# Another order of all engines' steps, from a search over four sets of transfer times

## The chip, the core and the metric

The kernel runs on one core of a Trainium2 chip. The metric is the device time of one execution in microseconds (us). The engines are TensorE (PE in the profile, its weight loads PEld), VectorE (DVE), ScalarE (ACT), GpSimd (POOL) and SyncE (SP), which here only issues transfers.

## What is computed

One transformer layer on x of 2048 rows by 512 columns, bf16: attention with 32 heads of 16 over a dilated window of 8 rows (the row itself and those 2, 4, ..., 14 before), then a gated feed-forward of width 1376, each behind a layer norm and with a residual.

```python
off = jnp.arange(W) * dil                     # W = 8, dil = 2
idx = pos[:, None] - off[None, :]             # rows before the first are masked
logits = jnp.einsum("bhsd,bhswd->bhsw", q, kg) * scale
attn = _softmax(jnp.where(mask, logits, -1e9), axis=-1)
o = jnp.einsum("bhsw,bhswd->bhsd", attn, vg)
...
h = x + _A_ref(_layernorm(x), A_wqkv, A_wo)
gate, up = hn @ W_gate, hn @ W_up             # hn = _layernorm(h)
h2 = h + (relu(gate) * up) @ W_down
```

## The kernel before, in words

The 2048 rows go in four chunks of 512 (0 to 3). For each chunk:

1. Layer norm of x, four blocks of 128 rows: statistics (L466, L469) on VectorE, the normalised rows on VectorE (L501) or ACT (L498). The rows are then transposed so that columns lie on the partitions: chunks 0 to 2 on TensorE (L530, evicted at L546), chunk 3 by four DMA transposes that SP issues (L519). The result is one `quad` buffer for each chunk.
2. Projections on TensorE (L571): twelve groups of four matmuls, 128x512 each, four groups for q, four for k and four for v, each evicted by ACT (L579).
3. Products of q and shifted k on VectorE (L619; in halves, L634, in chunk 0), their sums over a head's columns on TensorE (L625, 16 matmuls for a half, that is for four of the eight window rows), Exp on ACT (L683). In chunk 0 a mask is put on the weights' first columns (L686).
4. SP broadcasts a half's weights to all partitions in four transfers (L743, `big<-ex`). VectorE multiplies them with shifted v (L775; in halves, L790, in chunk 0) and adds the eight window rows in a tree. The first level of the tree, eight rows to four, is done in chunks 0 to 2 by an accumulating DMA that GpSimd issues (L818, 512 KB, `big<-big`), the others by VectorE (L778, L782 or L812).
5. Output projection on TensorE (L854; in chunk 0 the residual is added there, L857, and ACT evicts with a row sum, L863), layer norm of h (L447, L455, L501), feed-forward (L927, evicted at L931 and L934, products at L955) and down projection (L977) with the output. Chunks 0 and 1 add the residual by an accumulating DMA of GpSimd (L1011), 2 and 3 on VectorE (L990).

All four chunks overlap, so one engine's queue holds steps of several chunks. Every step is an `Op` with an engine. The table `RANK` has one number for each of the 744 steps; `Plan.order` sorts each engine's steps by it (SP's and GpSimd's too), and then replays the queues with assumed durations, one step at a time. Each engine thus executes its steps strictly by rank: where the next one must wait, all behind it wait. The assumed durations (of loads `XT` and `WT`, of engine operations `MM`, `SW`, `A5` and so on) no longer set the order within an engine. They only decide which of several equal buffers a step takes, the one that is assumed free first, and how the engines' steps stand among each other in the program's text.

Of the kernel before, what the change touches and what calls it, by code (L numbers as in the profile page):

```python
# [8 lines left out]
P = 128  # L9
# [3 lines left out]
ACT = mybir.ActivationFunctionType  # L13
ALU = mybir.AluOpType
# [188 lines left out]
def kernel(  # L203
# [11 lines left out]
    nc = tc.nc  # L215
    Bsz, S, D = A_x.shape
# [3 lines left out]
    NT = D // P  # L220
# [7 lines left out]
    PRD = ()  # L228
    ODA = (0, 1)
# [12 lines left out]
    HB = P // 4  # L242
# [53 lines left out]
    V = nc.vector  # L296
# [67 lines left out]
    add = plan.add  # L364
# [8 lines left out]
    TDD, TDL = 1.25, 1.5  # L373
    NWARM, NFILL = 56, (13, 10, 0)
    NHALF = 6
    XT = (3.55, 3.4, 6.1, 5.85, 9.0, 9.3, 9.6, 10.0, 15.2, 16.75)
    WT = (7.7, 7.7, 5.6, 12.05, 18.0, 24.95, 21.45, 28.8)
# [4 lines left out]
    BDI = {"S": 0.63, "A": 0.65, "P": 0.95}  # L382
# [16 lines left out]
    MM, TP = 0.2165, 0.057  # L399
    SW = 0.21  # L400
    PEL = 0.22
    A5, A10, AX, AS = 0.485, 0.91, 0.75, 0.21
    AL = 0.13
    D2, D5, D10, D20, D40, DST, DSM = 0.33, 0.61, 0.60, 1.14, 2.2, 0.61, 0.09
    DXN = 0.33
    DL = 0.12
# [147 lines left out]
    for tk in range(NCK):  # L554
# [50 lines left out]
        for hf in range(2):  # L605
            sc, ex = Buf(at_s), Buf(ex_s)
            scd, prd = [], []
            for t in range(0, NT, 2):
# [13 lines left out]
                def f_sc(t=t, sc=sc, pb=pb):  # L622
                    for u in range(2):
                        for g in range(4):
                            nc.tensor.matmul(sc.t[g * HB:(g + 1) * HB, :], lhsT=sel[:],  # L625
                                             rhs=pb.t[:, 4 * u + g, :], start=(t + u == 0),
                                             stop=(t + u == NT - 1), tile_position=(0, g * HB))
# [13 lines left out]
                else:  # L641
                    a = add(("pr%d" % hf, tk), "DVE", D40, f_pr, [d[k] for k in (t, t + 1) for d in (qd, kd, kp)],
                            apr, take=[pb], use=[qT], lat=DL)
                    prd.append((a, pb, f_sc))
# [29 lines left out]
            elif tk in MERGE:  # L674
                scd = [add(("sc%d" % hf, tk), "PE", 4 * MM + SW, lambda p=prd: [f() for _, _, f in p],
                           [a for a, _, _ in prd], apr, take=[sc], use=[b for _, b, _ in prd], lat=PEL)]
            else:
                for a, pb, f in prd:
                    scd.append(add(("sc%d" % hf, tk), "PE", 2 * MM + SW, f, [a] + scd[-1:], apr,
                                   take=[sc], use=[pb], lat=PEL))  # L680
# [52 lines left out]
        for w0 in range(0, W, BCN):  # L733
            hf = w0 // 4
            if (tk, hf) in BCD:
                for eng, q in (("SP", nc.sync), ("ACT", nc.scalar), ("POOL", nc.gpsimd)):
# [4 lines left out]
                    def f_bd(ws=ws, q=q, w0=w0, ab=ab, ex=exs[hf]):  # L741
                        for w in ws:
# [3 lines left out]
                                   take=[ab], use=[exs[hf]], lat=0.77,  # L746
# [102 lines left out]
        for j in range(BPC):  # L849
# [20 lines left out]
            if tk in RPE:  # L870
                a = add(("rs%d" % j, tk), "ACT", 0.57, f_rs, [a], base + 50, take=[sm], use=[od], lat=AL)
            else:
                a = add(("rs%d" % j, tk), "DVE", 0.63, f_rs, [a], base + 50, take=[sm], use=[od], lat=DL)
# [190 lines left out]
```

## Time and profile before

| what | us |
| --- | --- |
| median of 3 runs | 197.8 (197.04 to 198.03) |
| profiled execution (its span, from the first to the last instruction) | 199.0 |
| TensorE busy | 189.6 |
| VectorE busy | 147.9 |
| ACT busy | 116.7 |

The profiled execution is one run, 1.2 us over the median. In the views below, times are from the start of the span. A line such as `PE bank L571` is the work on TensorE that line 571 issues into a `bank` of PSUM. What stands in brackets behind a row of the timeline is the idle time ahead of it on its engine and what ended that. A busy TensorE in the profile is an upper bound, since a matmul's end is modelled. In a row of windows the busy times of PE, PEld, DVE, ACT and POOL follow each other, then the granted share of the TensorE clock, the share of DMA engines that were busy and GB/s.

### The profile page before, as it was taken

What the parts mean: (1) busy time and instruction counts of PE and PEld (TensorE: products, weight loads), DVE (VectorE), ACT (ScalarE), POOL (GpSimd) and SP (SyncE); (2) the same over time, 40 slices, a digit from 0 to 9 for tenths busy, and PEclk for the clock granted to TensorE, in tenths of its full rate; (3) what the DMA queues carried; (4) which work ended last, traced back from release to release, by engine and by line L of the source; (5) the groups of instructions that cost most, each with busy time, mean ns of one, the idle gap of its engine ahead of it and who ended that gap; (6) DMA issues with size and microseconds to landing.
All of it is one profiled execution on the core that took longest, in us unless ns stands there. A gap on an engine that the chain in (4) does not pass through costs nothing.

```text
span 199.0 us, 3083 instructions
## 1 busy us (share of the span) xinstructions
PE 189.6 (95%) x1120; PEld 98.5 (50%) x1139; DVE 147.9 (74%) x239; ACT 116.7 (59%) x241; POOL 17.7 (9%) x35
## 2 busy tenths in 40 slices
PE   8899998599999999999999999999999999999992
PEld 8895455245445534554444445544454544455451
DVE  6889999969969999999998769999954311214322
ACT  3579999326779676775536659606458725146300
POOL 3000002520000003300024010010010010000000
PEclk9999999879999999999999999999999999999999
DMA  6889386999600535967379973360030454000303
GB/s 207 231 274 381 96 183 126 190 187 350 217 0 0 137 78 105 190 127 160 80 146 174 188 174 65 65 120 3 0 53 8 103 178 110 0 0 0 109 6 126
DMA packets 25070, 24.61 MB, mean 124 GB/s; under 512 B 11136, under 2 KB 21344, under 8 KB 25056
## 3 DMA queue, kind: packets, MB, share of 16 engines
q1 hardware_dynamic: 22032, 16.23, 29.7%
q0 software_dynamic: 2304, 7.34, 20.2%
q10 hardware_dynamic: 720, 0.85, 1.2%
q8 instruction: 9, 0.15, 0.3%
q14 instruction: 5, 0.04, 0.1%
HBM read 8.42 MB, written 2.10 MB: 53 GB/s over the span
## 4 chain that ended last, share of the span: by engine, by line
PE 90%; DMA 5%; ACT 1%; issue 1%; DVE 1%; ACTq 0%
PE bank L927 34%; PE bank L571 20%; PE bank L977 19%; PE bank L854 7%; PE bank L625 4%; PE bank L894 3%; DMA quad<-row 3%; DMA x_sm<-in_A_x_dram 2%; PE bank L530 1%; ACT quad L579 1%; PE bank L857 0%; PE bank L700 0%; DVE st L466 0%; ACT lnd L706 0%; ACTq L319 0%
## 5 line engine op out<-in xcount | busy, mean ns | idle before, releaser
L927 PE MATMUL bank<-quad,wgu_sb 128*128 128x512 bf16 x311 | 72.0, 379 | 0.4
L927 PEld LDWEIGHTS <-wgu_sb 128*128 128x128 bf16 x320 | 31.0, 98 | 36.5 <-issue 0.8
L977 PE MATMUL bank<-wd_sb,gT 128*128 128x512 bf16 (+2 forms) x185 | 40.4, 367 | 0.2
L571 PE MATMUL bank<-quad,wqk_sb 128*128 128x512 bf16 (+1 forms) x149 | 31.2, 358 | 3.5 <-DMA quad<-row 3.1
L931 ACT CAST up_sb<-bank 128x512 bf16<-128x512 f32 x40 | 22.8, 589 | 19.5 <-PE bank L927 15.9
L934 ACT ACTIVATE gr<-bank 128x512 bf16<-128x512 f32 x40 | 23.3, 601 | 17.6 <-PE bank L927 10.9
L619 DVE TENSOR_TENSOR big<-quad,kT 128x4096 bf16<-128x4096 bf16 x12 | 27.2, 2284 | 2.4 <-ACT quad L579 2.2
L977 PEld LDWEIGHTS <-gT 128*128 128x128 bf16 (+1 forms) x187 | 18.1, 98 | 19.7 <-issue 0.4
L775 DVE TENSOR_TENSOR big<-big,vT 128x4096 bf16<-128x4096 bf16 x12 | 27.1, 2284 | 0.4 <-issue 0.2
L571 PEld LDWEIGHTS <-wqk_sb 128*128 128x128 bf16 x152 | 17.0, 115 | 15.1 <-issue 6.0
L955 DVE TENSOR_TENSOR gT<-gr,up_sb 128x1024 bf16<-128x1024 bf16 x20 | 13.7, 686 | 12.4 <-ACT up_sb L931 7.9
L990 DVE TENSOR_TENSOR row<-x_sm,bank 128x512 bf16<-128x512 bf16 (+1 forms) x9 | 5.5, 625 | 17.0 <-PE bank L977 17.0
L818 POOL DMA_DIRECT2D big<-big x12 | 10.5, 872 | 85.4 <-DVE big L775 59.8
L778 DVE TENSOR_TENSOR big<-big 128x1024 bf16<-128x1024 bf16 (+2 forms) x24 | 16.7, 728 | 0.8 <-DMA big<-big 0.8
L571 PE MATMUL bank<-quad,wv_sb 128*128 128x512 bf16 x61 | 15.7, 380 | 0.3 <-issue 0.2
L854 PE MATMUL bank<-wo_sb,quad 128*128 128x512 bf16 x62 | 14.9, 379 | 0.1
L579 ACT CAST vT<-bank 128x512 bf16<-128x512 f32 x16 | 9.0, 603 | 7.4 <-PE bank L571 7.4
L455 ACT ACTIVATE row<-x_sm,mv 128x512 bf16<-128x512 bf16 x12 | 8.5, 713 | 5.4 <-DVE mv L447 5.3
L466 DVE BATCH_NORM_STATS2 st<-x_sm 128x6 f32<-128x512 bf16 x16 | 10.3, 675 | 0.8 <-DMA x_sm<-in_A_x_dram 0.8
L546 ACT COPY quad<-bank 128x1024 bf16<-128x1024 bf16 (+1 forms) x10 | 8.5, 890 | 4.0 <-PE bank L530 4.0
L501 DVE TENSOR_SCALAR row<-x_sm,mv,rs 128x512 bf16<-128x512 bf16 x24 | 8.9, 406 | 2.5 <-ACT rs L483 2.5
L579 ACT CAST quad<-bank 128x512 bf16<-128x512 f32 x16 | 9.3, 593 | 2.3 <-PE bank L571 2.1
(77 smaller groups left out, 167.0 us busy)
## 6 DMA issues: line engine op xcount, KB each, us to landing
big<-big POOLq DMA_DIRECT2D x12, 512.0 KB, 5.4
big<-ex SPq DMA_DIRECT2D x32, 128.0 KB, 3.1
wgu_sb<-in_B_W_gate_dram SPq DMA_DIRECT2D x2, 688.0 KB, 9.2
wgu_sb<-in_B_W_up_dram SPq DMA_DIRECT2D x2, 688.0 KB, 6.0
wd_sb<-in_B_W_down_dram SPq DMA_DIRECT2D x2, 640.0 KB, 8.2
x_sm<-in_A_x_dram SPq DMA_DIRECT2D x2, 512.0 KB, 6.5
x_sm<-up_sb POOLq DMA_DIRECT2D x4, 256.0 KB, 3.4
out_dram<-x_sm SPq DMA_DIRECT2D x4, 256.0 KB, 3.1
```

Source lines behind the costliest of these rows:

```text
L571: nc.tensor.matmul(mm.t[:, lo:hi], lhsT=wv_sb[:, dt, t:D:NT] if c == 2 else wqk_sb[:, dt, c * D + t:(c + 1) * D:NT], rhs=xnT.t[:, dt, lo:h ...
L579: nc.scalar.copy(out=o, in_=mm.t[:])
L619: V.tensor_tensor(out=pb.t[:].rearrange("p (t w) s -> p t w s", t=2), in0=q4, in1=k4, op=ALU.mult)
L775: V.tensor_tensor(out=mt.t[:], in0=ab.t[:], in1=v8, op=ALU.mult)
L778: V.tensor_tensor(out=mt.t[:, 0:n, :], in0=mt.t[:, 0:n, :], in1=mt.t[:, n:2 * n, :], op=ALU.add)
L818: nc.gpsimd.dma_start(mt.t[:, 0:4, :], mt.t[:, 4:8, :], accum_op=ALU.add)
L854: nc.tensor.matmul(od.t[:], lhsT=OT.t[:, t, j * P:(j + 1) * P], rhs=wo_sb[:, t, :], start=(t == 0), stop=(t == NT - 1 and tk not in RPE))
L927: nc.tensor.matmul(mm.t[:fs, lo:hi], lhsT=wgu_sb[:, dt, g, ft * P: ft * P + fs], rhs=hnT.t[:, dt, lo:hi], start=(dt == 0), stop=(dt == NT ...
L931: nc.scalar.copy(out=ub.t[:fs, i, :], in_=um.t[:fs, :])
L934: nc.scalar.activation(out=gr.t[:fs, i, :], in_=gm.t[:fs, :], func=ACT.Relu)
L955: V.tensor_tensor(out=gt.t[:fs, 0:n, :], in0=gr.t[:fs, 0:n, :], in1=ub.t[:fs, 0:n, :], op=ALU.mult)
L977: nc.tensor.matmul(od.t[:, c0:c1], lhsT=gts[ft].t[:fs, ft % 2, j * P:(j + 1) * P], rhs=wd_sb[:fs, ft, c0:c1], start=(ft == 0), stop=(ft == ...
```

## The change

Nearly every entry of `RANK` is another number, from a search over four sets of assumed transfer times where the table before came from one. The tiles, the operations and their number on each engine stay: TensorE has 2280 instructions and ACT 228 rows in both, and no step is added, taken out or moved to another engine. With the table come other assumed durations, which act on the choice of buffers alone. Code for a further way to halve the products (`PRH`, `f_ph`) comes in, but `PRH` is empty, so it issues nothing.

```diff
 RANK = [
     0, 1, 2, 3, 4, 5, 6, 7, 8, 9, 10, 11, 12, 13, 14, 15, 16, 17, 18, 19,
-    20, 22, 23, 25, 28, 30, 31, 21, 24, 26, 27, 32, 35, 38, 40, 34, 39, 41, 43, 46,
+    20, 22, 23, 25, 29, 31, 32, 21, 24, 26, 28, 30, 36, 39, 40, 27, 33, 35, 37, 42,
...
+    PRH = {}
...
-    TDD, TDL = 1.25, 1.5
+    TDD, TDL = 1.3, 1.5
...
-    XT = (3.55, 3.4, 6.1, 5.85, 9.0, 9.3, 9.6, 10.0, 15.2, 16.75)
-    WT = (7.7, 7.7, 5.6, 12.05, 18.0, 24.95, 21.45, 28.8)
+    XT = (3.47, 3.64, 5.45, 5.97, 8.4, 8.7, 9.25, 9.75, 15.9, 17.65)
+    WT = (7.65, 7.65, 5.0, 13.7, 19.0, 24.95, 22.4, 28.8)
...
-    BDI = {"S": 0.63, "A": 0.65, "P": 0.95}
+    BDI = {"S": 0.66, "A": 0.67, "P": 0.95}
...
-    MM, TP = 0.2165, 0.057
-    SW = 0.21
+    MM, TP = 0.216, 0.056
+    SW = 0.115
...
-                    for u in range(2):
+                hs = PRH.get((tk, hf, t))
+                def f_sc(t=t, sc=sc, pb=pb, hs=hs):
+                    for u in range(1 if hs else 2):
...
-                                             stop=(t + u == NT - 1), tile_position=(0, g * HB))
+                                             stop=(t == NT - 2 and bool(u or hs)), tile_position=(0, g * HB))
...
-                                   take=[ab], use=[exs[hf]], lat=0.77,
+                                   take=[ab], use=[exs[hf]], lat=0.97 if tk else 1.2,
```

Since lines are added, a line number of the change is higher than that of before: by 1 from L229, by 3 at L634, by 13 from L686 on.

VectorE, chunk 0, the products of q and k (`big<-quad,kT`) and the masks (`ex<-ex,mask`). Before:

```order
L634 TENSOR_TENSOR big2_90<-quad1_80,kT_77 128x2048
L634 TENSOR_TENSOR big3_91<-quad1_80,kT_77 128x2048 x2
L634 TENSOR_TENSOR big0_88<-quad1_80,kT_77 128x2048
L686 TENSOR_TENSOR ex0_100<-ex0_100,mask_65 128x16
L466 BN_STATS st0_114<-x_sm_71 128x6
```

And with the change:

```order
L637 TENSOR_TENSOR big0_88<-quad1_80,kT_77 128x2048
L637 TENSOR_TENSOR big3_91<-quad1_80,kT_77 128x2048
L699 TENSOR_TENSOR ex0_100<-ex0_100,mask_65 128x16
L637 TENSOR_TENSOR big3_91<-quad1_80,kT_77 128x2048
L467 BN_STATS st0_114<-x_sm_71 128x6
```

The first mask, on which the first four broadcasts of SP wait, stands ahead of the last of the eight products. The scores and the Exp that it needs have moved forward on TensorE and ACT: ahead of the scores TensorE now does two groups of v in place of three, and four small transposes of chunk 1 in place of sixteen.

VectorE a little later, the products with v (`big<-big,vT`) and the statistics of chunk 2 (`mv3`). Before:

```order
L466 BN_STATS st2_116<-x_sm_71 128x6
L790 TENSOR_TENSOR big1_89<-big4_92,vT_78 128x2048
L469 BN_AGGR mv3_121<-st2_116 128x2
L469 BN_AGGR mv3_121<-st0_114 128x2
L469 BN_AGGR mv3_121<-st1_115 128x2
L469 BN_AGGR mv3_121<-st3_117 128x2
L790 TENSOR_TENSOR big2_90<-big4_92,vT_78 128x2048
L790 TENSOR_TENSOR big1_89<-big4_92,vT_78 128x2048
L501 TENSOR_SCALAR row2_107<-x_sm_71,mv3_121,rs3_133 128x512
```

And with the change:

```order
L467 BN_STATS st3_117<-x_sm_71 128x6
L470 BN_AGGR mv3_121<-st2_116 128x2
L470 BN_AGGR mv3_121<-st0_114 128x2
L470 BN_AGGR mv3_121<-st1_115 128x2
L470 BN_AGGR mv3_121<-st3_117 128x2
L803 TENSOR_TENSOR big1_89<-big4_92,vT_78 128x2048
L803 TENSOR_TENSOR big2_90<-big4_92,vT_78 128x2048
L803 TENSOR_TENSOR big0_88<-big4_92,vT_78 128x2048 x2
L502 TENSOR_SCALAR row4_109<-x_sm_71,mv3_121,rs3_133 128x512
```

The first accumulating DMA of GpSimd reads and writes the buffer whose two halves are complete first. That is `big1` after the third product before, and `big0` after the fourth with the change. On SP the order around it stays: eight broadcasts, then the four transposes of chunk 3.

ACT behind the transposes of chunk 2 (`quad5`). `quad4` is the q of chunk 1, `quad6` and `quad8` those of chunks 3 and 2. Before:

```order
L546 COPY quad5_84<-bank7_141 128x4x256
L709 ACTIVATE rec0_104<-lnd0_103 128x512
L579 CAST kT_77<-bank5_139 128x512
L579 CAST vT_78<-bank2_136 128x512
L579 CAST quad6_85<-bank3_137 128x512
L579 CAST quad4_83<-bank0_134 128x512
```

And with the change:

```order
L547 COPY quad5_84<-bank7_141 128x4x256
L580 CAST vT_78<-bank2_136 128x512
L580 CAST quad4_83<-bank4_138 128x512
L580 CAST kT_77<-bank1_135 128x512
L580 CAST kT_77<-bank5_139 128x512
L722 ACTIVATE rec0_104<-lnd0_103 128x512
L580 CAST vT_78<-bank0_134 128x512
L580 CAST quad6_85<-bank3_137 128x512
```

The last q of chunk 1 stood behind a v and a q of chunk 3 and now stands ahead of chunk 3's first q.

Further on, the second half of chunk 2's scores moves on TensorE. Between it and the second half of chunk 1's scores stood six groups of projections, one output projection of chunk 0, a sum of weights and sixteen small transposes; now two groups stand there. The scores of chunk 1 in turn stand behind all four output projections of chunk 0 in place of three.

More of the change, by code (lines that the diff above doesn't have):

```diff
@@ L396 @@
     LNA = ((0, 1, 0, 1), (0, 0, 0, 0))
-    MM, TP = 0.2165, 0.057
-    SW = 0.21
+    MM, TP = 0.216, 0.056
+    SW = 0.115
     PEL = 0.22
-    A5, A10, AX, AS = 0.485, 0.91, 0.75, 0.21
+    A5, A10, AX, AS = 0.48, 0.905, 0.72, 0.21
     AL = 0.13
@@ L620, in f_pr @@
                                     in0=q4, in1=k4, op=ALU.mult)
-                def f_sc(t=t, sc=sc, pb=pb):
-                    for u in range(2):
+                hs = PRH.get((tk, hf, t))
+                def f_sc(t=t, sc=sc, pb=pb, hs=hs):
+                    for u in range(1 if hs else 2):
                         for g in range(4):
@@ L643, with f_ph @@
                             apr, take=[pb], use=[qT], lat=DL)
+                    if hs == "D":
+                        def f_ph(pb=pb):
+                            nc.gpsimd.dma_start(pb.t[:, 0:4, :], pb.t[:, 4:8, :], accum_op=ALU.add)
+                        a = add(("ph%d" % hf, tk), "POOL", 1.0, f_ph, [a], apr, use=[pb], lat=1.1, dq=(0.75, 2.74))
+                    elif hs:
+                        def f_ph(pb=pb):
+                            V.tensor_tensor(out=pb.t[:, 0:4, :], in0=pb.t[:, 0:4, :], in1=pb.t[:, 4:8, :], op=ALU.add)
+                        a = add(("ph%d" % hf, tk), "DVE", D20, f_ph, [a], apr, use=[pb], lat=DL)
                     prd.append((a, pb, f_sc))
@@ L674 @@
             elif tk in MERGE:
-                scd = [add(("sc%d" % hf, tk), "PE", 4 * MM + SW, lambda p=prd: [f() for _, _, f in p],
+                scd = [add(("sc%d" % hf, tk), "PE", (4 - sum((tk, hf, t) in PRH for t in (0, 2))) * MM + SW, lambda p=prd: [f() for _, _, f in p],
                            [a for a, _, _ in prd], apr, take=[sc], use=[b for _, b, _ in prd], lat=PEL)]
@@ L870 @@
             if tk in RPE:
-                a = add(("rs%d" % j, tk), "ACT", 0.57, f_rs, [a], base + 50, take=[sm], use=[od], lat=AL)
+                a = add(("rs%d" % j, tk), "ACT", 0.575, f_rs, [a], base + 50, take=[sm], use=[od], lat=AL)
             else:
-                a = add(("rs%d" % j, tk), "DVE", 0.63, f_rs, [a], base + 50, take=[sm], use=[od], lat=DL)
+                a = add(("rs%d" % j, tk), "DVE", 0.73, f_rs, [a], base + 50, take=[sm], use=[od], lat=DL)
             hd.append((a, od))
```

72 rows, old and new, of the table RANK are left out of this document.

## The prediction

> **What bounds the kernel now.** I read the page's busy shares first, then TensorE's waits, then the chain that ended last, then the stage in which the one long wait lies.
>
> Busy shares (page), and TensorE's waits by what ended them:
>
> ```profile
> PE 189.6 (95%) x1120; PEld 98.5 (50%) x1139; DVE 147.9 (74%) x239; ACT 116.7 (59%) x241; POOL 17.7 (9%) x35
> ```
>
> ```profile
> PE bank L571 <- DMA quad<-row: 3.1, 1, 3.1
> ```
>
> TensorE is the bound: in 199.0 us it waits for one thing only, apart from the start and the end. No instruction is added or removed by the change, so the time can move by waits alone. Pieces of the chain (start, length, what):
>
> ```profile
> 18.71 0.67 PE bank L530 x12
> ...
> 31.79 5.28 DMA quad<-row
> 37.07 0.14 issue
> 37.20 5.09 PE bank L571 x15
> ...
> 60.22 2.59 PE bank L571 x12
> ```
>
> A projection matmul costs 2.59/12 = 0.216 us when the stream runs, a group of four 0.86; twelve small transposes cost 0.67. Around 37 us, 15 of them take 5.09. Windows of the same place (length, busy by engine, granted clock, DMA):
>
> ```profile
> 33.90:37.20 3.30, 0.24 (x5) 0.09 (x3) 3.30 (x4) 2.77 (x4) 0.86 (x1) 1.00 1.07 205
> 37.20:42.34 5.14, 5.09 (x15) 2.12 (x17) 5.14 (x7) 0.00 (x0) 2.86 (x3) 0.67 1.03 193
> ```
>
> So the wait costs twice: 3.06 us of idleness (0.24 busy in 3.30), and then a granted clock of 0.67 over 5.14 us, 0.33 x 5.14 = 1.70 us. Together **4.76 us**. After 37 the order of before hardly loses anything on TensorE.
>
> What is late? The four DMA transposes of chunk 3 on SP's queue, and of them the last. Timeline:
>
> ```profile
> 27.77 5.24 SPq L519 DMA_TRANSPOSE quad<-row  x4
> ...
> 31.64 1.01 POOL L818 DMA_DIRECT2D big<-big  x1 [21.61 <-PE bank L571]
> ...
> 31.79 1.22 SPq L519 DMA_TRANSPOSE quad<-row  x1
> ...
> 33.30 0.84 PE L530 MATMUL bank<-identity,row 128*128 128x128 bf16 x12
> ```
>
> From issue to landing, of the four:
>
> ```profile
> DMA to landing us min/median/max: 2.4/2.6/5.3
> ```
>
> The 5.3 is the fourth (5.28 in the chain). It was issued 0.15 us after GpSimd's first accumulating transfer (512 KB, L818). With 2.4 to 2.5 it would have landed at 31.79 + 2.45 = 34.24, about when TensorE ran out (33.30 + 0.84 = 34.1). Packets by queue, first all of 31.6 to 33.4 (none of the software queue), then that queue's from 33.4 to 33.7:
>
> ```profile
> q1 hardware_dynamic: 774, 0.19, 53.0%
> ```
>
> ```profile
> q0 software_dynamic: 7, 0.03, 57.6%
> ```
>
> The accumulate's first packets run 1.8 to 2.0 us after its issue. The transpose needs 2.45 to land. So a transpose is safe when the accumulate is issued at least 2.45 - 1.8 = 0.65 us after it; here it came 0.15 before. A later pair is a control:
>
> ```profile
> 98.41 2.51 SPq L519 DMA_TRANSPOSE quad<-row  x2
> ```
>
> ```profile
> 100.88 0.86 POOL L818 DMA_DIRECT2D big<-big  x1 [17.02 <-DVE big L775]
> ```
>
> ```profile
> DMA to landing us min/median/max: 2.4/2.5/2.5
> ```
>
> The second of these is issued at about 99.66, 1.2 us ahead of the accumulate, and lands in 2.5 at most.
>
> **The change, part by part. (1) The transposes go earlier.** They stand on SP behind eight broadcasts (L743), four for each half of the softmax weights, and each four wait for their mask on VectorE (L686):
>
> ```profile
> 21.63 6.04 SPq L743 DMA_DIRECT2D big<-ex  x8
> ```
>
> ```profile
> 13.47 8.03 DVE L634 TENSOR_TENSOR big<-quad,kT 128x2048 bf16<-128x2048 bf16 x7
> 21.43 0.17 DVE L686 TENSOR_TENSOR ex<-ex,mask 128x16 bf16<-128x16 bf16 x1
> ...
> 23.97 0.15 DVE L686 TENSOR_TENSOR ex<-ex,mask 128x16 bf16<-128x16 bf16 x1
> ...
> 27.18 1.23 DVE L790 TENSOR_TENSOR big<-big,vT 128x2048 bf16<-128x2048 bf16 x1 [0.41 <-DMA big<-ex]
> 28.32 0.37 DVE L469 BATCH_NORM_AGGREGATE mv<-st 128x2 f32<-128x6 f32 x4
> 28.61 2.42 DVE L790 TENSOR_TENSOR big<-big,vT 128x2048 bf16<-128x2048 bf16 x2
> ```
>
> A half product occupies VectorE for 8.03/7 = 1.14 us. The first mask moves ahead of the eighth product: 21.43 - 1.14 = 20.29, and the first four broadcasts with it (0.75 each: 20.5 to 23.5). The second mask keeps its place (product and mask only swap), ending at 24.12. In before, SP was still issuing the first four until 21.63 + 6.04/2 = 24.65; now it is free, so the second four start at 24.15, 0.5 earlier, end at 27.2, and the fourth transpose is issued at about 27.25 + (31.79 - 27.77) = **31.25**.
>
> **(2) The accumulate goes later.** In before it follows three products with V, the last ending at 28.61 + 2.42 = 31.03; it starts 0.6 later. Now four products stand ahead of it, and the four BN_AGGR ahead of those: VectorE was free at 27.18 - 0.41 = 26.77; + 0.3 = 27.05, + 4 x 1.14 + 0.08 = 31.7. The 0.41 us for which it waited for a broadcast is gone, as the first four are 1.1 us earlier. With 0.3 (a quick wake) to 0.6 us, the accumulate is issued at **32.0 to 32.3**, 0.75 to 1.05 after the fourth transpose. That lies between -0.15 (disturbed) and 1.2 (undisturbed), above the 0.65 worked out from the packets, by 0.1 to 0.4 us. I take it as undisturbed: landing at 31.25 + 2.45 = 33.7, and TensorE asks for chunk 3 at 34.1 less what (3) gives. Term: **-3.06** for the wait, bounds -3.06 and 0.
>
> The clock goes with the wait: **-1.70**, bounds -1.70 and 0. [...]
>
> **(3) The start.** VectorE waited for the fourth block of x, whose statistics stood ahead of the third's:
>
> ```profile
> 5.98 0.69 DVE L466 BATCH_NORM_STATS2 st<-x_sm 128x6 f32<-128x512 bf16 x1 [0.48 <-DMA x_sm<-in_A_x_dram]
> ```
>
> Taking the third block first, issued on the other queue at the same time, wins at most 0.48, and loses what that one lands later, if it does; I take **-0.3**, bounds -0.48 and +0.2.
>
> **(4) Scores are asked for sooner.** TensorE's first scores (L625) stand behind two groups of V in place of three, and behind four small transposes in place of sixteen:
>
> ```profile
> 19.32 1.05 PE L625 MATMUL bank<-big,sel 128*32 128x512 bf16 x16
> ```
>
> 19.32 - 0.86 - 0.67 = 17.8, less 0.3 from (3): 17.5. They need five products, which end at 13.47 + 4 x 1.14 + 0.08 = 18.1, earlier by as much as the first product is (0 to 0.48). So TensorE idles 0.1 to 0.6: **+0.4**. That is the price of (1).
>
> **(5) Behind 37 us** VectorE and ACT have to keep up with a TensorE that is 4.4 us earlier. On ACT two evictions of chunk 3 held the last q of chunk 1 behind them; now chunk 1's stand ahead. VectorE's waits from 42 to 60, and the busy times after:
>
> ```profile
> DVE big L619 <- ACT quad L579: 2.2, 1, 2.2
> DVE mv L447 <- ACT x_sm L863: 2.1, 1, 2.1
> ```
>
> ```profile
> 60.00:100.00 40.00, 39.79 (x248) 18.86 (x251) 39.60 (x52) 27.51 (x60) 3.44 (x4) 1.00 0.53 111
> ```
>
> VectorE (the third busy time) has 2.2 + 2.1 us of waits there, both caused by a late TensorE, plus the 0.41 of (2): 4.7, against 4.66 that TensorE wins. From 60 to 100 it is full (39.60 of 40). So it can just follow. I allow **+0.3** for waits of a few tenths, bounds 0 and 2.1 (the second wait stays). The output at the end is 0 either way.
>
> Sum: 199.0 - 3.06 - 1.70 - 0.3 + 0.4 + 0.3 = **194.6 us** of span, -4.4. The median shown, 197.8, is 0.6% under the profiled 199.0, so I take the difference over: 197.8 - 4.4 = **193.4 us**. Half a per cent (1.0 us) is about what a measurement can tell.
>
> **The rivals.** *VectorE becomes the bound.* If the 2.1 us for the sums of h stay, because its own chain is that late, TensorE wins 2.1 less: 195.5. For: it is full from 60 to 100. Against: that wait ended with TensorE's own output projection, which comes earlier.
>
> *The order doesn't do what it says.* The accumulate still meets the fourth transpose: 0.1 to 0.4 us of margin is small, and the broadcasts can be slow. Then 3.06 and 1.70 stay, and (3) to (5) give +0.1 to +0.4: 198.0. [...]
>
> *The other side: scores of chunk 2 on TensorE.* In before their second half had room:
>
> ```profile
> 59.05 2.28 DVE L619 TENSOR_TENSOR big<-quad,kT 128x4096 bf16<-128x4096 bf16 x1
> ```
>
> ```profile
> 66.44 1.05 PE L625 MATMUL bank<-big,sel 128*32 128x512 bf16 x16
> ```
>
> Their product ended at 61.33, 5.1 us ahead. Now two groups of projections stand between the scores of chunk 1 and these, where there were six, one output projection (5 x 0.216 = 1.08), sixteen small transposes and a sum, 7.4 us in all; and the output projection has gone ahead of both. 7.4 - 1.7 - 1.1 = 4.6 us earlier. So 0.5 is left, and VectorE's lateness beyond that goes straight onto TensorE. It decides from about 3 us on: then the clock is lost too (1.70), and with 4.5 us late the sum is 194.6 + 4.0 + 1.7 = 200.3, 199.1 as a median. For: that VectorE is full. Against: the 4.7 us of its waits that go.
>
> **How the numbers follow.** Forecast 0.62 (193.4; 192.4 to 194.4 by the bounds of (3) to (5)), VectorE bound 0.16 (195.5), transpose still disturbed 0.15 (198.0), scores late 0.07 (199.1). The range, 192.3 to 197.9, leaves out about 0.05 below, and above half of the third case and the fourth, 0.15. Faster by over 0.5% (under 196.8): the first two and a little of the third, 0.79. Within 0.5%: most of the third, 0.13. Slower: 0.08.
>
> **What would show it.** Right: no TensorE wait on the transposes of chunk 3, clock 1.00 from 30 to 45, the fourth landing about 2.5 us after its issue, the first accumulate issued 0.7 us or more behind it, scores at about 18 with a gap of some tenths. Wrong: a landing over 3 us, a dip of the clock, or TensorE waiting for VectorE near 57.

## The result, and the profile after

| | executions | median us | range us |
| --- | --- | --- | --- |
| before | 20 | 197.81 | 196.44 to 200.17 |
| after | 20 | 196.63 | 195.57 to 197.69 |

The ratio is 0.9937, with a 95% interval of 0.9918 to 0.9957. The change makes the kernel 1.2 us faster, where the forecast was 4.4 us. Ratios, here and below, leave out executions that took over 1.5% longer than the fastest of the same kernel. The span of the profiled execution of the changed kernel is 193.7 us, and its own time 196.0 us.

In that profile nearly every step went as forecast. Busy shares (page) and TensorE's waits by what ended them:

```profile
PE 188.5 (97%) x1120; PEld 99.0 (51%) x1139; DVE 147.2 (76%) x239; ACT 115.2 (59%) x241; POOL 17.4 (9%) x35
```

```profile
PE bank L421 <- DVE warm L322: 1.0, 1, 1.0
```

The 3.1 us for `quad<-row` are gone from the waits; what is left is the start of the program. In this kernel L520 is the DMA transpose that was L519, L831 the accumulate that was L818, L756 the broadcasts that were L743. The two windows of the forecast (length, busy by engine, clock, DMA):

```profile
33.90:37.20 3.30, 3.25 (x21) 1.84 (x20) 3.30 (x4) 3.00 (x5) 0.86 (x1) 1.00 1.00 189
37.20:42.34 5.14, 5.14 (x26) 2.68 (x25) 4.84 (x8) 3.56 (x8) 2.71 (x4) 1.00 1.04 195
```

TensorE is busy for 3.25 of 3.30 us where it had 0.24, and the clock behind it is 1.00 where it was 0.67. The four transposes of chunk 3 on SP, the first accumulate on GpSimd, the products ahead of it, and the transposes' time to landing:

```profile
26.62 5.23 SPq L520 DMA_TRANSPOSE quad<-row  x4
26.97 4.63 DVE L803 TENSOR_TENSOR big<-big,vT 128x2048 bf16<-128x2048 bf16 x4
32.21 1.01 POOL L831 DMA_DIRECT2D big<-big  x1 [22.18 <-DVE row L502]
```

```profile
DMA to landing us min/median/max: 2.4/2.5/2.7
```

The last transpose is issued at 30.64, the accumulate at 32.21, 1.57 us behind it, and that transpose lands in 2.4 us. So the mechanism of the forecast is there, and the 4.76 us that it names are gone from the profile: 199.0 to 193.7. But the medians differ by 1.2. The experiments ask why.

### The profile page after: what moved, and what is told of

It reads as the page before. It is cut to its first block, busy times and chain, and to the rows that moved or that the text cites. A ratio compares the mean times of both kernels' runs of the same rounds, so it can differ in the third digit from the quotient of the medians.

```text
span 193.7 us, 3083 instructions
## 1 busy us (share of the span) xinstructions
PE 188.5 (97%) x1120; PEld 99.0 (51%) x1139; DVE 147.2 (76%) x239; ACT 115.2 (59%) x241; POOL 17.4 (9%) x35
## 4 chain that ended last, share of the span: by engine, by line
PE 97%; ACT 1%; issue 1%; DVE 0%; ACTq 0%
PE bank L940 35%; PE bank L572 21%; PE bank L990 20%; PE bank L867 7%; PE bank L628 4%; PE bank L421 3%; PE bank L907 3%; PE bank L531 2%; PE bank L429 1%; ACT up_sb L944 1%; PE bank L870 0%; PE bank L713 0%; PE bank L716 0%; DVE row L1003 0%; ACT vT L580 0%
## 5 line engine op out<-in xcount | busy, mean ns | idle before, releaser
L990 PE MATMUL bank<-wd_sb,gT 128*128 128x512 bf16 (+2 forms) x185 | 39.6, 366 | 0.1
L944 ACT CAST up_sb<-bank 128x512 bf16<-128x512 f32 x40 | 22.3, 590 | 22.2 <-PE bank L940 20.5
L572 PE MATMUL bank<-quad,wqk_sb 128*128 128x512 bf16 (+1 forms) x148 | 29.4, 344 | 0.3
L831 POOL DMA_DIRECT2D big<-big x12 | 10.5, 904 | 81.7 <-DVE big L788 54.2
L878 DVE SCALAR_TENSOR_TENSOR x_sm<-x_sm,bank 128x512 bf16<-128x512 bf16 x12 | 8.2, 687 | 4.9 <-PE bank L867 4.7
L580 ACT CAST kT<-bank 128x512 bf16<-128x512 f32 x16 | 9.1, 597 | 3.3 <-PE bank L572 1.8
```

What stands on the lines that cost most here:

```text
L572: nc.tensor.matmul(mm.t[:, lo:hi], lhsT=wv_sb[:, dt, t:D:NT] if c == 2 else wqk_sb[:, dt, c * D + t:(c + 1) * D:NT], rhs=xnT.t[:, dt, lo:h ...
L580: nc.scalar.copy(out=o, in_=mm.t[:])
L831: nc.gpsimd.dma_start(mt.t[:, 0:4, :], mt.t[:, 4:8, :], accum_op=ALU.add)
L944: nc.scalar.copy(out=ub.t[:fs, i, :], in_=um.t[:fs, :])
L990: nc.tensor.matmul(od.t[:, c0:c1], lhsT=gts[ft].t[:fs, ft % 2, j * P:(j + 1) * P], rhs=wd_sb[:fs, ft, c0:c1], start=(ft == 0), stop=(ft == ...
```

## The experiments

The table `RANK` is edited in single entries. Names of steps: mu3a and mu3c are the products with V that the first accumulate (ta3) waits for, mu0c and mu1c belong to other accumulates. The diffs name the steps in place of their positions in the table. Ratios are to the kernel before on the same chip. The kernel before ran 122 times beside these kernels.

### Both kernels again, and the accumulate moved in each

Two kernels are unchanged. In the other two VectorE's products are put in another order:

```diff
 # order of before, accumulate later
-RANK: mu3a 163, mu1a 175; tree3 203, pr1 of chunk 1 206
+RANK: mu1a 163, mu3a 175; pr1 of chunk 1 203, tree3 206
 # changed order, accumulate earlier
-RANK: mu1c 150, mu0c 155, mu3c 160, mu3a 166
+RANK: mu3c 150, mu0c 155, mu3a 160, mu1c 166
```

> The order of before, unchanged, profiled once more. Theory A (every execution of before loses the 4.8 us that its first profile shows): span about 199, fourth transpose of chunk 3 landing over 5 us after its issue, granted clock under 1.00, and all timed executions with a clock of about 0.99. Theory B (the profiled execution was an unusual one, and the median execution loses far less there): span 194 to 197, and most executions with a clock of 1.00. Time: equal to before, by either.

> The order of before with four entries exchanged on VectorE alone: the second product of head group 3 with V changes places with the first of group 1, so that the first accumulate is issued some 1.6 us later, 1.5 us after the fourth transpose in place of 0.15 before it; and the first tree step of group 3 changes places with the next product of q and k, which hides the later landing. Theory A: the transpose lands in 2.5 us, and the median falls by 4 to 4.8 us, to 193.0 to 193.8. Theory B: the transpose lands in 2.5 us as well, but the median falls by 0 to 1.5 us only.

> The change with three entries exchanged on VectorE alone: the two products of head group 3 with V stand one place earlier, so that the first accumulate is issued about 1.1 us earlier, 0.35 us after the fourth transpose or a little more in place of 1.6. By the margin of 0.65 us worked out in the prediction the transpose is disturbed. Theory A: landing over 5 us after the issue, clock under 1.00, and the median 4 us over that of the change. Theory B: disturbed in some executions only, the median 0 to 1.5 us over that of the change, with a wider spread.

> The change, unchanged, profiled once more, to see what differs between two executions of one order. Both theories: 0.994 of before, all executions with a clock of 1.00, spans of 193.3 to 195.4.

| | median us | ratio (95%) | profiled span, clock | accumulate behind the last transpose | it lands in |
| --- | --- | --- | --- | --- | --- |
| before again | 197.62 | 0.9983 (0.9951 to 1.0015) | 195.9, 0.998 | 0.45 | 2.7 |
| before, accumulate later | 197.76 | 1.0014 (0.9982 to 1.0045) | 197.2, 0.999 | 2.27 | 2.4 |
| after, accumulate earlier | 196.95 | 0.9959 (0.9932 to 0.9987) | 194.6, 0.999 | 0.37 | 3.2 |
| after again | 196.84 | 0.9948 (0.9917 to 0.9979) | 193.3, 1.0 | 1.41 | 2.4 |

In the changed order an accumulate 1 us earlier makes the transpose land in 3.2 us, and the time is within 0.1 us of the changed kernel's. In the order of before, keeping the accumulate away from the transposes wins nothing. That run alone doesn't settle it, since the edit costs something elsewhere: its profile has a wait of 0.4 us at 52 us that before again does not have. The reason is in the second profile of the unchanged kernel: TensorE's waits, then from the timeline the first v product, the accumulate and the transposes, and their time to landing.

```profile
PE bank L530 <- DVE row L501: 1.7, 2, 1.4
PE bank L420 <- DVE warm L321: 1.0, 1, 1.0
PE bank L571 <- ACT rs L479: 0.3, 1, 0.3
PE bank L571 <- issue: 0.2, 1, 0.2
```

```profile
28.77 5.26 SPq L519 DMA_TRANSPOSE quad<-row  x4
28.89 1.23 DVE L790 TENSOR_TENSOR big<-big,vT 128x2048 bf16<-128x2048 bf16 x1 [1.04 <-DMA big<-ex]
...
33.25 1.01 POOL L818 DMA_DIRECT2D big<-big  x1 [22.24 <-DVE row L501]
```

```profile
DMA to landing us min/median/max: 2.4/2.6/2.8
```

There is no wait for the transposes. VectorE's first v product waited 1.04 us for a broadcast, against the 0.41 that the prediction shows. So the accumulate came 0.45 us behind the last transpose and not 0.16 ahead of it, and that transpose landed in 2.7 us. The collision of the profiled execution hangs on one broadcast that came some 0.6 us early.

How rare is that? Of each timed execution the span and the mean clock are recorded. The collision took 1.70 us of clock, 0.9% of a span, and gave a mean of 0.991. Of the 122 executions of the kernel before, three have a mean clock at or below 0.991; they took 201.05, 201.40 and 201.51 us (spans 199.2 to 199.7), while half of all lie under 197.6. None of the three was traced in detail. That they are collisions is inferred from the clock and the span alone, and these do not prove it: the kernel `apart` of the last experiment, whose accumulate comes over 4 us behind the transpose, has one execution with a mean clock of 0.991 too. A collision that costs a wait but no clock is not in the count. In 36 further executions with this order of accumulate and transposes (before again, and the variants "third block first" and "x first" below) there are three more such clocks; in 75 of the changed kernel and its variants with the same accumulate there is none under 0.997.

### The first layer norm's third and fourth block

The new waits above lie at the start, for the block of x that VectorE takes third. The order of before takes the fourth block there, the changed order the third. Each kernel got the other's order of these two, on every engine, and nothing else:

```diff
 # order of before (the changed order: the other way round)
-RANK: xst3 29, xag3 33, xxn3 42, xtp3 47, ...; xst2 34, xag2 39, xxn2 46, xtp2 49, ...
+RANK: xst2 29, xag2 33, xxn2 42, xtp2 47, ...; xst3 34, xag3 39, xxn3 46, xtp3 49, ...
```

> The kernel before, with one thing changed: in the first layer norm the third block of x goes ahead of the fourth on every engine, as after the change (statistics, rsqrt, normalise, transposes, evictions), nothing else. Theory S (most of the real 1.2 us lies at the start: VectorE's normalise of the second block stands in its queue behind the statistics of the fourth block of x, which landed at 6.0, 7.1 and 7.1 us in three profiles of before, so that the first projection began at 8.3, 9.4 and 9.4 us, against 8.0 to 8.6 in three profiles of the changed kernel): VectorE's third group starts at 5.6 to 5.8 us, the first projection at 8.0 to 8.6, the time is 196.6 to 197.0 us, a ratio of 0.994 to 0.997 to before. Theory R (the gain lies behind the start, in the order from 34 us on and in the stores at the end): ratio 0.999 to 1.001, 197.6 us, wherever the first projection starts.

> The changed kernel, with the fourth block of x ahead of the third in the first layer norm again, as before the change, nothing else. Theory S: the wait for the late fourth block is back, the first projection starts at 8.3 to 9.4 us, and the time loses most of the gain: 197.4 to 197.7 us, a ratio of 0.998 to 1.000 to before. Theory R: 196.7 to 197.0 us, a ratio of 0.994 to 0.996, as the changed kernel itself.

Measured: before with the third block first 197.69 us, 1.0004 (0.998 to 1.0029); after with the fourth block first 196.53 us, 0.9957 (0.9937 to 0.9977). Theory S falls on both sides. When a block of x lands differs from one execution to the next with the same order: in the two profiles of the unchanged kernel before, the third group of statistics began at 5.98 and at 7.06 us. The timeline's row of the third group of statistics, in before with the third block first, and in before again:

```profile
6.02 0.69 DVE L481 BATCH_NORM_STATS2 st<-x_sm 128x6 f32<-128x512 bf16 x1 [0.59 <-DMA x_sm<-in_A_x_dram]
```

```profile
7.06 0.69 DVE L466 BATCH_NORM_STATS2 st<-x_sm 128x6 f32<-128x512 bf16 x1 [1.87 <-DMA x_sm<-in_A_x_dram]
```

Before with the third block first is also the nearest control of the collision. Its first projection came at 8.37, as in the profile that the forecast used (8.32), and its last transpose at 31.81 (31.79 there). But the v product waited longer:

```profile
27.88 1.23 DVE L805 TENSOR_TENSOR big<-big,vT 128x2048 bf16<-128x2048 bf16 x1 [1.07 <-DMA big<-ex]
...
32.24 1.01 POOL L833 DMA_DIRECT2D big<-big  x1 [21.86 <-DVE row L516]
```

The accumulate is 0.43 behind the transpose, which landed in 2.7 us, and the span is 194.8. In the profiled execution of before SP had issued the fourth broadcast at 24.05, here at 24.49. What held SP is not settled.

### The loads of x first

If late blocks of x are chance, they can be taken out of both kernels. The four loads of x are issued ahead of the four weight loads, where they alternated:

```diff
                 q.dma_start(x_sm[:, j:j + 1, :], x_rows[:, j:j + 1, :])
+        for i in range(2):
+            for n, q in enumerate((nc.sync, nc.scalar)):
+                j = 2 * i + n
                 q.dma_start(wqk_sb[:, j:j + 1, :], w3_r[:, j:j + 1, 0:2 * D])
```

> The changed kernel, with the four loads of x issued ahead of the four loads of the q and k weights on the two queues, in place of alternately. Theory S: x lands by 4.5 us in every execution, VectorE waits for no third or fourth block, the first projection starts at 7.7 to 8.2 us whenever it runs, the spread of the times falls, and the median is 196.0 to 196.5 us, a ratio of 0.991 to 0.994 to before. Rival (the start is set by the warm matmuls and the weights): the weights now land last, the first or the second group of projections waits for them, and the time is 196.7 us or more.

> The changed kernel with the loads of x ahead of the weights' loads, once more, beside the changed kernel on the same chip. If the late blocks of x set the start: first projection at 7.6 to 7.7 us again (it was 7.65), against 8.0 to 8.9 without it, and a median 0.3 to 0.8 us below that of the changed kernel, ratio 0.990 to 0.994 to before. Rival (the spread of the start doesn't carry through to the end): the two medians within 0.2 us.

> The changed kernel unchanged, as the yardstick of the other three: a ratio of 0.994 to 0.996 to before as in the earlier runs, first projection at 8.0 to 8.9 us, 187.5 to 187.7 us from there to the end; the four transposes of chunk 3 land in 2.4 to 2.8 us.

> The kernel before, with the loads of x ahead of the weights' loads; the order of the steps is that of before. Theory P (the gain of the change lies behind the first projection): the first projection comes at 7.6 to 8.4 us, 188.2 to 188.4 us from there to the end as in the other profiles of before, time 196.5 to 197.0 us, a ratio of 0.994 to 0.997 to before, and 0.6 to 0.8 us above the changed kernel with the same loads. Theory Q (the gain lies at the start): with the start made equal the two kernels with x first are within 0.3 us of each other, this one at 195.9 to 196.3 us.

> The changed kernel with the loads of x ahead of the weights' loads, beside the kernel before with the same loads. First projection at 7.6 to 8.4 us, 187.6 to 187.9 us from there to the end, time 195.8 to 196.3 us, a ratio of 0.990 to 0.994 to before, in either theory.

| | median us | ratio (95%) | first projection | from there to the end of the time |
| --- | --- | --- | --- | --- |
| after, x first | 196.17 | 0.9926 (0.9900 to 0.9951) | 7.65 | 187.9 |
| after, x first (2nd) | 195.90 | 0.9921 (0.9895 to 0.9948) | 8.27 | 187.8 |
| after, beside the 2nd | 196.47 | 0.9941 (0.9916 to 0.9966) | 9.10 | 187.6 |
| before, x first | 197.24 | 0.9963 (0.9937 to 0.9989) | 7.85 | 189.6 |
| after, x first (3rd), beside it | 196.37 | 0.9917 (0.9884 to 0.9950) | 8.37 | 187.9 |

The last column is the profiled execution's own time less the start of its first projection. The wait for the third group is gone, as in the first of these:

```profile
5.01 0.38 DVE L507 TENSOR_SCALAR row<-x_sm,mv,rs 128x512 bf16<-128x512 bf16 x1
5.31 0.69 DVE L472 BATCH_NORM_STATS2 st<-x_sm 128x6 f32<-128x512 bf16 x1
```

With the same loads the two orders are 0.9 us apart (197.24 and 196.37), and that although the order of before had the earlier first projection in its profile. Each of the six executions of the one was faster than each of the twelve of the other. Theory Q falls, and what theory P says holds, that the gain lies behind the first projection; its numbers for the order of before do not (189.6 us where 188.2 to 188.4 were expected, and 197.24 where 196.5 to 197.0 were). Without x first the order of before takes 188.3 us from the first projection to the end (before again, and third block first), the changed order 187.5 to 187.7 (four profiles). With x first the order of before loses 1.3 us of its earlier start again. TensorE's waits there, behind the start, are

```profile
PE bank L535 <- DVE row L506: 0.5, 2, 0.3
PE bank L576 <- ACT kT L584: 0.3, 1, 0.3
```

They are 0.8 us between 30 and 35 us, where before again has 0.3 and the changed order none; the rest of the 1.3 us no wait shows. After with x first is the fastest version here. Against before that is certain; against the changed kernel it is 0.57 us in the one direct comparison, and the intervals overlap. But its 19 executions lie between 195.5 and 196.6 us, the changed kernel's between 195.6 and 197.9. Its first projection did not come at 7.6 to 7.7 us each time, as was expected, but at up to 8.37: something other than x holds the start too (see the last section).

### Half of the new order

Can the gain be put to a stage? The first 200 steps or so (to 37 us) in one kernel's order, the rest in the other's:

```diff
-RANK = the order of before (or the changed one) for all 744 steps
+RANK = one order's first 200 (202) steps, then all other steps by the other order
```

> The changed order for the first 200 steps (to about 37 us), the order of before for the other 544. In the profiled runs, the time from the first projection to the end was 188.3 us for the kernel before (two profiles, 197.71 - 9.41 and 196.67 - 8.37) and 187.5 to 187.7 us for the changed kernel (three profiles). Theory H (these 0.7 us lie ahead of 37 us: TensorE's short waits near 20 and 34 us, 0.5 us in before and none after): 187.6 to 187.9 us from the first projection to the end, no wait of TensorE over 0.15 us behind the start, a ratio to before of 0.994 to 0.997. Theory T (they lie behind 37 us, in the feed-forward and the stores at the end): 188.1 to 188.3 us, a ratio of 0.998 to 1.000.

> The order of before for the first 202 steps (to about 37 us), the changed order for the other 542. Theory H: 188.1 to 188.3 us from the first projection to the end, the two waits near 20 and 34 us still there, a ratio of 0.998 to 1.000. Theory T: 187.6 to 187.8 us, a ratio of 0.994 to 0.997.

Measured: changed order first 197.57 us, 0.9998 (0.9974 to 1.0022); changed order behind 197.98 us, 1.0021 (0.9997 to 1.0045). From the first projection to the end 188.9 and 189.3 us. Both are longer than either theory said (187.6 to 188.3), and the second ratio is above both forecasts. TensorE's waits, first the one and then the other:

```profile
PE bank L531 <- DVE row L502: 0.6, 2, 0.4
```

```profile
PE bank L531 <- DVE row L502: 1.6, 2, 1.3
PE bank L940 <- ACT quad L547: 0.8, 1, 0.8
```

With the changed order ahead, the waits at 20 and 34 us are gone, but one of 0.4 us stands at 61.0; with it behind, 0.8 us stand at 65.1. From the first projection to the end the two take 1.3 and 1.7 us more than the changed kernel; the waits shown behind the start are 0.4 and 1.2 us of that. My reading is that at the seam each half meets a state that its own order didn't prepare; no run tests it. This cut doesn't divide the gain, and whether another would is open.

### The collision on purpose

First mu3a went straight behind mu3c in the order of before:

```diff
-RANK: mu3c 148, xag.2 152 154 155 156, mu0c 157, mu3a 163
+RANK: mu3c 148, mu3a 150, xag.2 152 154 155 156, mu0c 157
```

> The kernel before, with VectorE's two v products that the first accumulating DMA waits for next to each other, so that GpSimd issues this DMA 1.1 us earlier, 0.7 to 1.3 us ahead of the last of the four DMA transposes of chunk 3 in place of 0.15 us ahead (profiled execution of before) or 0.5 us behind (its second profile). Theory of the collision as predicted: a transpose issued after the accumulate lands in 5.0 to 5.5 us in place of 2.5, TensorE idles 2.5 to 3.5 us near 34 us and has half its clock for some us more, span 199 to 201 us with a mean clock of 0.991, time 200 to 202 us, a ratio of 1.015 to 1.025, in most executions. Rival (the late landing in the profiled execution had another cause, chance among it): all four transposes land in 2.3 to 3.2 us, and the time is that of before, 197.4 to 197.9 us.

Measured: 199.48 us, 1.0088 (1.0057 to 1.0120); the accumulate came 0.11 us ahead of the last transpose, which landed in 5.2 us. The time lies between the two theories, and the price of the collision can't be read from it. TensorE's waits and a row of ACT's timeline:

```profile
PE bank L573 <- ACT kT L581: 1.7, 1, 1.7
PE bank L532 <- DVE row L503: 1.5, 1, 1.5
PE bank L573 <- ACT quad L548: 1.3, 1, 1.3
```

```profile
32.55 0.30 ACT L481 ACTIVATE rs<-mv,eps_t 128x4 f32<-128x4 f32 x1 [2.47 <-DVE mv L471]
```

The product, which itself waited 0.56 us for a broadcast, stood ahead of VectorE's four BN_AGGR, and ACT's rsqrt with all its evictions waited 2.47 us for these. The 1.7 us on TensorE come from there. The 1.3 us, which ended at 38.30, have two causes at once: ACT's copy, late for the same reason, ended at 38.22, and the late transpose landed at 38.17. The other 1.5 us are the late block of x.

So mu3a was put behind the BN_AGGR, and in a second kernel ta3 behind another accumulate, with the sums that need it later. Order on SP, ACT and TensorE is that of before in both:

```diff
 # together
-RANK: mu0c 157, mu3a 163
+RANK: mu3a 156.5, mu0c 157
 # apart: this, and
-RANK: ta3 171, ta1 192; tree3 203 and 212, om3 216, lg 220
+RANK: ta1 192, ta3 192.5; tree3 221.3 and 221.5, om3 221.7, lg 222
```

> The kernel before, with the second of the v products that the first accumulate waits for put one product earlier on VectorE, behind the four BN_AGGR this time, so that ACT isn't held back; the accumulate is issued up to 0.6 us earlier, within 0.15 us of the last transpose of chunk 3. Theory of the collision: that transpose lands in 5.0 to 5.5 us, TensorE waits 2.5 to 3.1 us for chunk 3 near 34 to 37 us and then runs at half clock for 3 to 4 us, span 198.5 to 200, time 200.3 to 201.8 us. Rival (something else holds TensorE there anyway): the transpose is late, but TensorE waits less than 1 us and the time stays at 197.5 to 198.3 us.

> The same, but GpSimd issues that accumulate as its second, behind another one, at 36 to 37 us, and VectorE's sums that need it stand three steps later. Theory of the collision: the four transposes land in 2.4 to 2.8 us, no wait of TensorE over 0.5 us near 34 us, clock 1.00, time 197.5 to 198.2 us, 2.5 to 4 us below the run with the two together. Rival: the same time as that run, within 0.5 us.

| | median us | ratio (95%) | accumulate behind the last transpose | it lands in |
| --- | --- | --- | --- | --- |
| together | 199.27 | 1.0098 (1.0073 to 1.0124) | -0.05 | 4.3 |
| apart | 200.33 | 1.0163 (1.0131 to 1.0194) | 4.33 | 2.4 |

TensorE's waits, together and then apart:

```profile
PE bank L532 <- DVE row L503: 1.7, 3, 0.8
PE bank L422 <- DVE warm L323: 1.0, 1, 1.0
PE bank L573 <- DMA quad<-row: 0.8, 1, 0.8
```

```profile
PE bank L537 <- DVE row L508: 2.3, 3, 1.2
PE bank L861 <- DVE quad L789: 1.5, 1, 1.5
...
PE bank L632 <- DVE big L626: 0.6, 1, 0.6
```

The wait for `quad<-row` is there with the two together, and gone apart, so it is the accumulate that makes the transpose late. It is only 0.8 us, since TensorE was already 1.1 us late for other rows, and the transpose was late by 1.9 and not 2.8. The totals say nothing on the price, and neither theory's times came: apart was to be 2.5 to 4 us faster than together, or the same, and is 1.1 us slower, with waits of 1.5 and 0.6 us at 52 to 55 us that together doesn't have. It moved the accumulate and the sums behind it too late, as I read it. A collision that costs TensorE the whole 3.06 us and the clock of 0.67 was seen in detail in one execution only, the one that the forecast used.

## Why the prediction was right or wrong

**The failed step is the last line of the sum**: "so I take the difference over: 197.8 - 4.4". It takes the profiled execution for a usual one because 199.0 is only 0.6% above the median of 197.8. But one is a span and the other a time. In the 122 executions of the kernel before recorded later, the time is 1.8 to 1.9 us more than the span. The profiled execution was therefore, as an estimate, some 200.8 us long, 3 us above the median, and above all three runs shown. The usual execution has a span of 195.7 (the median of 122). Its second traced execution and that of the third-block variant do not meet the collision, and by clock and span hardly any of the 122 does: 4.76 us of stall cannot be taken out of a median that doesn't contain them.

**The sum in spans came out, in part by luck.** It said 194.6. The median span of the changed kernel's 20 executions is 194.35, its profiles show 193.3 to 194.4. Set on the right footing, 194.6 plus the 2.3 us by which time and span differ in that kernel is 196.9, against 196.63 measured. (The 2.3 is known only from these runs; with the 1.8 of the kernel before it would be 196.4.) It was the footing of before that was wrong, by 3 us. The luck is in the small terms: together they were to add 0.4 us and none of them is seen, while the span from the first projection to the end fell by 5.4 us in the two profiles, 0.7 more than the 4.76.

**The terms**, in the profile of after:

- The transposes earlier (1): last one forecast at 31.25, issued at 30.64. Right in kind, but 1.15 us earlier than before where about half a us was forecast: the second four broadcasts took 2.6 us to issue, from 24.04, and not 3.0 (0.75 each).
- The accumulate later (2): forecast 32.0 to 32.3, issued at 32.21. The margin is 1.57 where 0.75 to 1.05 was forecast. The needed margin of 0.65, worked out from packets, is borne out: nothing is left of the delay from 0.56 on (last section).
- -3.06 and -1.70: gone in the profile, as forecast. In the usual execution, as far as it was traced, they weren't there to gain. That a wait takes clock with it, one profile shows: behind the 3.06 us of before the granted clock is 0.50 from 38.5 to 41.5 us. In the first run of the collision on purpose waits of 1.66 and 1.29 us left it at 1.00 from 31 to 39 us. Where between these the loss begins no run shows; "from about 3 us on" in the last rival is an estimate from the one wait.
- The start (3), -0.3: no effect that these runs can see, between -0.4 and +0.6 us by the interval of the swap in before. VectorE's wait is 0.44 for the third block, where it was 0.48 for the fourth. In this profile it did not matter: TensorE has no wait ahead of its first projection.

```profile
5.62 0.69 DVE L467 BATCH_NORM_STATS2 st<-x_sm 128x6 f32<-128x512 bf16 x1 [0.44 <-DMA x_sm<-in_A_x_dram]
```

- Scores asked for sooner (4), +0.4: too much. They come at 17.9, as forecast, but TensorE is busy up to there, with four small transposes between the projections and the scores.

```profile
15.87 1.89 PE L572 MATMUL bank<-quad,wv_sb 128*128 128x512 bf16 x8
17.60 0.39 PE L531 MATMUL bank<-identity,row 128*128 128x128 bf16 x4
17.92 1.05 PE L628 MATMUL bank<-big,sel 128*32 128x512 bf16 x16
```

- Behind 37 us (5), +0.3: 0. TensorE has no wait over 0.15 us there.

**What the forecast didn't have** is the gain that the usual execution does get. Of its 1.2 us, 0.7 can be read from the profiles of both orders, as the time from the first projection to the end. Most of that are two short waits of the order of before, 0.17 us near 21 and 0.30 near 34 us, which before again and its third-block variant have and the changed order has not; some 0.1 us is the end, where the order of before issues the store of a block of chunk 2 just ahead of the last one. The prediction had "after 37 the order of before hardly loses anything", which holds. Ahead of 37 it passed over the 0.17, and the 0.30 does not stand in the profile that it used. The remaining 0.5 us are within what the start scatters from one execution to the next, and no run puts them to a place.

**The rivals.** VectorE did not become the bound, and the scores of chunk 2 (57.1 us) waited for nothing. The transposes are not disturbed in the changed order: all four land in 2.4 to 2.8 us in its three profiles. The rival that was missing: that the profiled execution is not the one that the median measures.

## What to carry to other kernels

Before a stall of one profiled execution goes into a sum, put that execution on the scale of the timed ones: its own time, not its span, against the median and its spread, and its mean clock against theirs. A stall that makes the profiled run longer than every timed run is to be taken for an event, not a cost, until a second profile of the same kernel shows it again. Where a stall hangs on the order in which two engines issue transfers by some tenths of a us, ask from execution to execution which comes first.

## What was not expected of the hardware

**How late the transpose is follows from the gap of issues.** Over the profiles of both orders and their variants:

| accumulate issued behind the last transpose, us | its landing, us |
| --- | --- |
| -0.16 / -0.11 / -0.05 | 5.3 / 5.2 / 4.3 |
| 0.37 | 3.2 |
| 0.43 / 0.45 / 0.50 | 2.7 / 2.7 / 2.6 |
| 0.56 to 4.33 (eleven profiles) | 2.4 |

Some 0.7 us of order decides over 2.8 us of delay, with nothing left from 0.56 on. Which part of the transpose the accumulate holds up, no run here shows.

**Time less span is nearly constant for a kernel and differs between kernels**: 1.8 to 1.9 us in all executions of the kernel before, 2.2 to 2.35 in those of the changed kernel, and 1.8 to 1.9 again with the changed order and the accumulate earlier. Part of the shorter span (193.7 against 195.9) is therefore no gain in time. Spans of two kernels should not be compared to less than half a us without the times.

**The start scatters for two reasons.** The third group of statistics could begin at 5.6 to 7.3 us from the same issues of loads. With x loaded first it began at 5.3 to 5.4, and the spread of the changed kernel's times fell; that of the kernel before did not (196.6 to 200.7 us with x first). The other reason is on TensorE. The 56 matmuls that it does ahead of the first transposes (`warm`) took 4.6 to 5.8 us. The same kernel, after and after again:

```profile
0.99 5.68 PE L421 MATMUL bank<-warm 128*128 128x128 bf16 x56 [0.99 <-DVE warm L322]
```

```profile
0.99 4.87 PE L421 MATMUL bank<-warm 128*128 128x128 bf16 x56 [0.99 <-DVE warm L322]
```

In the profiles of before and after these matmuls start some 107 ns apart at first and some 56 ns apart later; the change falls at 4.26 us in before and at 6.03 us in after, where in each trace the first record of the granted clock, 1.00, stands. In five profiles, that of after and two of the three of the changed kernel with x first among them, TensorE had no wait ahead of its first projection, so there this and not x set the start. Both together moved the first projection between 7.65 and 9.62 us.
